# A new written order for the first nineteen steps of attention + MoE on one core, with two products moved to other banks

## The chip, the cores and the metric

The kernel runs on one core of a Trainium2 chip. The time is device microseconds (us) of one execution; the number given for a kernel is the median of its runs. A profile is one execution with the hardware profiler on; its span runs from the first instruction to the last. PE is the matmul engine (PEld its weight loads), DVE the vector engine, ACT the scalar engine with its tables, POOL the general one, SP the engine that only issues DMAs here.

## The reference

```python
def _attn_ref(q, k, v):                       # (8, 8, 576, 64) each
    q_s = softmax of q over the last axis
    k_s = softmax of k over the sequence
    kv = np.einsum('bhsd,bhse->bhde', k_s, v)
    return np.einsum('bhsd,bhde->bhse', q_s, kv)
def _moe_ref(x, w_in, w_out):                 # x: the result above as (4608, 512); w_in (512, 2048), w_out (2048, 512)
    h = x @ w_in
    g = h - np.tanh(h)
    return g @ w_out
```

Both softmaxes subtract the maximum first and divide by the sum + 1e-9. The weights come in 64 bit floats (512 KB for a 128-row piece) and are decoded on the chip.

## The kernel before

The 4608 rows of x are worked in nine chunks of 512. For each chunk j and each of 16 slices f of d_ff there is a **step** (j, f): a product `ph` = x times a slice of w_in (12 matmuls of 128x512, since x and the weight are split into a high and a low part: xh·wh, xl·wh, xh·wl), then the function of it, then `po`, the product of its result with a slice of w_out into four sums of 128 rows (12 matmuls, 3 for each sum), two steps later. The first steps are (0, 0) to (0, 7), then (1, 0) to (1, 15); step number n in the order's names is (0, n) for n < 8, else (1, n - 8). The sums of chunk 0 over its first eight slices are put aside in DRAM (`ev` copies a sum to SBUF, `sv` stores it) and taken up again later.

PSUM has eight banks here: four for the sums (`ps_o`, tag "o"), two for the products `ph` (`ps_h`, tag "h"), two for the rest (`ps_m`, tag "m"). Each pool hands its banks out in turn, so a tile waits until all readers of the tile that had its bank are done. Until the sums begin, the four banks of `ps_o` hold the first transposes and the first `px`.

Around the products stand small operations, one engine each:

- a step: `u`, `t`, `vv`, `m` (the mask `mk`), `gh` on ACT; `g`, `tt`, `gg`, `cp` on DVE; `gl` on POOL, or on DVE with a star in the order. `u`, `t`, `m`, `g`, `tt` read the product's bank.
- a weight piece, w_in (`i`) or w_out (`o`): `ld` is its load (SP), `cl` and `st` on DVE, `pr`, `lo` and `ca` on ACT, `sub` (the low part) on POOL, or on DVE with a star.
- k and v of a batch: loads `k`, `v` (the 512 KB pieces of v are filled with ones by POOL first), column maximum `km` on DVE, `pm` (transpose, PE), `mx`, `mh`, `ml` (DVE), `pb` (PE), `ks` (subtract, DVE), `ke` (exp, ACT), `pk` (PE), `sl`, `rs`, `rc`, `kn` (DVE), which gives `kvs`.
- a piece of q: load `q`, `mq` (maximum, DVE), `qu` (subtract, POOL), `qe` (exp, ACT), `sq` (sum, DVE), `sa`, `sr`; then per 128 rows `qn` (POOL), `pt` (transpose, PE), `qs` (copy, ACT), and per pair `px` (PE), whose parts `xh` (ACT) and `xl` (DVE) are x.

`warmN` is N idle matmuls on the identity. The string ORDER lists all of this for the first 17 steps, batches 0 and 1 and all 32 weight pieces, in one list; each engine executes its entries in that order, and its instructions wait only by semaphores. From step 17 on loops write the steps, PE and SP in order and the others as a scheduler orders them; batch 2's k and v are worked among the last steps of ORDER.

Of the kernel before, what the change touches and what calls it, by code (L numbers as in the profile page):

```python
# [29 lines left out]


ORDER = """
k0.0 warm13 k0.1 q1 km0.a k0.2 km0.b q0 km0.c mq1 v0.1 km0.d qu1 pm0 v0.2 mq0 warm16 v0.0 mx0
qu0 qe1 ld.i0 sq1 qe0 ld.o0 mh0 sa1 ml0 sr1 pb0 sq0 qn2 ld.i2 warm1 lo.i0 qn3 ks0.0 pt2 warm1
qs2 sa0 pt3 ks0.1 ke0.0 ld.i1 warm2 qs3 ks0.2 pk0.0 ke0.1 sr0 ld.i3 cl.i0 qn0* pr.i0 pk0.1 cl.i2
ke0.2 st.i0 pr.i2 ld.o2 pt0 cl.i1 ca.i0 qn1 pk0.2 lo.i2 warm1 sl0 sub.i0 pr.i1 ld.i4 rs0 pt1 rc0
qs0 warm2 kn0 qs1 cl.i3 px2 lo.i1 cl.o0 ld.o1 st.i2 pr.o0 px0 st.i1 xh2.1 cl.o2 xh2.0 xl2.1
ld.i5 ca.i1 warm11 xl2.0 xh0.1 xh0.0 sub.i1* ca.i2 xl0.1 ld.o3 lo.o0 sub.i2 xl0.0 pr.i3 ph0
lo.i3 k1.0 cl.o1 lo.o1 st.o0 lo.i4 st.i3 ca.o0 cl.i4 ld.o4 cl.o3 ca.i3 sub.o0* pr.i4 ph1 sub.i3*
u0 st.i4 k1.2 t0 ld.i6 vv0 g0 m0 tt0 ca.i4 gg0 ph2 v1.0 u1 sub.i4 t1 g1 vv1 tt1 lo.o2 ld.i7 gg1  # L40
pr.o2 cp0 u2 st.o2 pr.o1 k1.1 cl.i6 gh0 st.o1 m1 gl0* t2 ph3 q3 cp1 ca.o2 ca.o1 cl.i5 sub.o2*
gh1 sub.o1 g2 pr.i5 ld.o5 tt2 m2 po0 t3 gl1* vv2 v1.2 km1.a pr.i6 v1.1 gg2 pr.o3 km1.b u3 ph4
cp2 lo.o3 ld.o6 g3 lo.i5 st.o3 gh2 lo.i6 st.i5 q2 ca.o3 gl2* po1 ca.i5 st.i6 vv3 sub.i5* ld.o7
ca.i6 gg3 m3 sub.o3 tt3 lo.i7 mq3 ld.i8 po2 lo.o5 sub.i6 u4 mq2 t4 vv4 ld.i9 qu3 g4 lo.o4 ph5
tt4 lo.o7 lo.o6 ld.o8 cp3 qe3 km1.c gh3 cl.o4 ld.o12 km1.d m4 t5 sq3 gl3 ph6 pr.o4 ld.o11 u5 tt5
lo.i9 cl.i7 lo.i8 gg4 ld.o13 pr.i7 st.o4 po3 vv5 cp4 ca.o4 st.i7 ld.i12 gh4 qu2* u6 m5 pm1 gl4*
qe2 ld.i11 mx1 ca.i7 sub.o4* t6 sq2 sub.i7 po4 ld.o9 lo.o11 lo.i12 g5 lo.o8 mh1 cl.o5 lo.o13
ld.o10 ml1 gg5 pr.o5 sa2 pb1 sa3 cp5 vv6 sr2 ld.i10 lo.i11 sr3 ph7 qn5 ks1.0 gh5 m6 gl5 ks1.1
ke1.0 ld.i13 ks1.2 lo.o9 qn6 pk1.0 ke1.1 tt6 qn7 g6 pt6 ke1.2 pk1.1 qs6 st.o5 ld.o15 t7 qn4*
ca.o5 pt5 cl.o6 pk1.2 u7 sub.o5* qs5 ld.i15 sl1 gg6 po5 pr.o6 rs1 lo.i13 cp6 vv7 rc1 st.o6 gh6  # L50
kn1 ca.o6 cl.o7 pt4 m7 g7 sub.o6 pt7 qs4 tt7 qs7 gl6* pr.o7 px6 lo.o15 gg7 lo.i15 st.o7 po6
ld.i14 xh6.0 cp7 xh6.1 xl6.0 gh7 xl6.1 ca.o7 gl7* lo.o10 px4 sub.o7* lo.i10 lo.o12 cl.i8 cl.i9
po7.0 xh4.1 ld.o14 cl.o8 xh4.0 cl.o9 po7.1 xl4.1 pr.i8 xl4.0 pr.i9 po7.2 st.i8 pr.o8 ph8 st.i9
ev.1 ca.i8 cl.o11 sv.1 cl.i11 ca.i9 sub.i8 pr.i11 lo.o14 po7.3 sub.i9* t8 ph9 cl.i13 u8 tt8 m8
g8 vv8 cl.i10 ev.3 gg8 pr.i10 sv.3 cl.o14 ev.2 cp8 ph10 t9 sv.2 st.i10 gh8 tt9 m9 gl8* u9 pr.o14
st.o8 po8.0 t10 g9 vv9 po8.1 tt10 u10 gg9 ph11 ca.o8 g10 vv10 cp9 pr.o9 gg10 gh9 sub.o8* m10
po8.2 gl9* t11 ph12 u11 cp10 ev.0 g11 m11 sv.0 tt11 vv11 cl.o12 ca.i10 gg11 pr.o11 po8.3
sub.i10* u12 ph13 cp11 gh10 st.o11 vv12 gl10* m12 st.i11 t12 pr.o12 g12 po9 t13 tt12 u13 gg12
ca.i11 tt13 vv13 sub.i11 lo.i14 ph14 gh11 cp12 ca.o11 gl11 m13 pr.i13 sub.o11 g13 po10 u14 t14
gg13 tt14 vv14 cp13 ph15 st.o12 gh12 cl.i14 m14 gl12* ca.o12 cl.o15 pr.i14 g14 pr.o15 st.i14  # L60
po11 u15 gg14 t15 sub.o12* ca.i14 cp14 vv15 tt15 m15 ph16 sub.i14* gh13 cl.i12 gl13* pr.i12
st.o14 g15 ca.o14 po12 st.i12 t16 u16 gg15 ca.i12 sub.o14 tt16 vv16 cp15 gh14 sub.i12 m16 gl14*
st.o15 po13 g16 ca.o15 gg16 cl.o10 cp16 po14 gh15 cl.o13 sub.o15 pr.o10 pr.o13 gl15* st.o10 gh16
st.o13 ca.o10 gl16 ca.o13 sub.o13* sub.o10* st.o9 cl.i15 ca.o9 pr.i15 sub.o9 st.i15 st.i13
ca.i15 ca.i13 sub.i15 sub.i13
"""


# [1 line left out]
def attn_moe_kernel(  # L70
# [113 lines left out]

# [351 lines left out]
    po = {}

    def h_mm(j: int, f: int):
        xh, xl = xs[j]
        ph = ps_h.tile([P, CH], F32, name=f"ph{j}_{f}", tag="h")  # L540
        w = wt["i", f].rearrange("p t (c f) -> p t c f", c=NC)
        ops = [(i, x, c) for i, x in ((0, xh), (0, xl), (1, xh)) for c in range(NC)]
        for n, (i, x, c) in enumerate(ops):
            nc.tensor.matmul(  # L544
                ph, w[:, i, c], x[:, c, :], start=(n == 0), stop=(n == len(ops) - 1)
            )
# [281 lines left out]
```

## Time and profile before

| | |
|---|---|
| median of 3 runs | 918.2 us (917.87 to 918.79) |
| the profiled execution | 920.28 us, span 918.5 us |
| PE busy | 890.2 us (97%) |
| DVE, ACT, POOL busy | 615.4, 556.1, 288.2 us |
| first product `ph0` begins | 30.52 us into the span |
| `po16` ends, `ph19` begins | 159.45 us |
| weight pieces, q, k, v | 512 KB loads, 256 KB for each store of 128 rows |

In the rows of the profile, the name ahead of "<-" is what is written, behind it what is read, buffer numbers left out; xN is the number of instructions. In a table by stretches each engine has its busy us and, in brackets, its instructions; then follow the clock that PE was granted (1.00 is full), the DMA engines' share and GB/s. In a list of waits the columns are the total, the number and the longest, in us. A timeline row starts with the start and the length in us, and the bracket at its end holds the idle time before it and what ended it.

### The profile page before, as it was taken

The page shows a single profiled execution, that of the slowest core. Times are in us where ns is not written, and L with a number is a line of the kernel's source. Part 1 is how long each engine was busy: PE and PEld are TensorE (multiplying, and loading weights), DVE is VectorE, ACT ScalarE, POOL GpSimd, SP SyncE. Part 2 cuts the span into 40 slices and gives each one's busy share as a digit, 9 for nine tenths or more (in the row PEclk, how much of TensorE's full clock was granted, in tenths as well). Part 3 has the DMA queues.
Part 4 walks back from the last instruction along what each step waited for, and adds up shares of the span by engine and source line. Part 5 has one row for each costly group of instructions (what it writes and reads, how often), then busy time and mean ns, then how long its engine had stood idle before and what let it go on. Part 6 is the DMA issues. An engine that isn't in the chain of part 4 may idle for free.

```text
span 918.5 us, 13209 instructions
## 1 busy us (share of the span) xinstructions
PE 890.2 (97%) x5034; PEld 721.9 (79%) x5034; DVE 615.4 (67%) x906; ACT 556.1 (61%) x967; POOL 288.2 (31%) x246
## 2 busy tenths in 40 slices
...
GB/s 254 317 305 118 95 82 1 9 61 92 1 126 47 103 1 58 115 12 24 46 61 67 24 46 24 115 0 16 79 24 1 1 70 12 0 1 46 1 1 46
DMA packets 79776, 57.47 MB, mean 63 GB/s; under 512 B 14689, under 2 KB 72033, under 8 KB 79713
## 3 DMA queue, kind: packets, MB, share of 16 engines
...
q8 instruction: 39, 0.64, 0.3%
q14 instruction: 25, 0.20, 0.1%
...
## 4 chain that ended last, share of the span: by engine, by line
PE 77%; DVE 7%; ACT 5%; DMA 4%; issue 4%; POOL 2%; SPq 0%; DVEq 0%; ACTq 0%; POOLq 0%
PE po L635 37%; PE ph L544 35%; PE pk L299 2%; DMA k<-in_k_dram 2%; PE px L465 1%; PE pt L437 1%; DVE g L573 1%; DVE g L565 1%; DVE g L578 1%; DMA spare_q<-in_q_dram 1%; ACT gh L581 1%; DVE t L570 1%; DMA raw_o<-in_moe_w_out_dram 1%; POOL d L267 1%; DMA q<-in_q_dram 1%
## 5 line engine op out<-in xcount | busy, mean ns | idle before, releaser
L635 PE MATMUL po<-w_o,gh 128*128 128x512 f32 x1152 | 361.5, 395 | 1.5 <-DVE w_o L167 1.5
L544 PE MATMUL ph<-xh,w_i 128*128 128x512 f32 x1152 | 317.7, 398 | 10.3 <-ACT mk L559 6.0
L584 POOL TENSOR_TENSOR gl<-g,gh 128x512 fp32r<-128x512 f32 x130 | 172.6, 1328 | 389.7 <-ACT gh L581 373.5
L544 PEld LDWEIGHTS ph<-xh,w_i 128*128 128x128 f32 x1152 | 214.6, 190 | 59.3 <-ACT mk L559 7.3
L635 PEld LDWEIGHTS po<-w_o,gh 128*128 128x128 f32 x1152 | 214.7, 188 | 51.0 <-DVE w_o L167 1.8
L565 DVE SCALAR_TENSOR_TENSOR g<-u,ph 128x512 f32<-128x512 f32 x144 | 98.3, 682 | 219.2 <-ACT t L559 202.2
L635 PE MATMUL po<-w_o,gl 128*128 128x512 f32 x576 | 226.4, 393 | 1.5 <-DVE gl L584 1.5
L581 ACT CAST gh<-g 128x512 fp32r<-128x512 f32 x144 | 89.2, 620 | 177.7 <-DVE g L578 172.6
L544 PE MATMUL ph<-xl,w_i 128*128 128x512 f32 x576 | 157.9, 397 | 0.0
L559 ACT ACTIVATE u<-ph 128x512 f32<-128x512 f32 x144 | 85.8, 596 | 81.4 <-PE ph L544 81.1
L573 DVE SCALAR_TENSOR_TENSOR g<-vv,g 128x512 f32<-128x512 f32 x144 | 120.4, 836 | 20.0 <-ACT vv L559 10.4
L544 PEld LDWEIGHTS ph<-xl,w_i 128*128 128x128 f32 x576 | 109.8, 191 | 25.0 <-DVE xl L486 0.6
L635 PEld LDWEIGHTS po<-w_o,gl 128*128 128x128 f32 x576 | 108.1, 188 | 27.0 <-DVE gl L584 2.4
L578 DVE COPY_PREDICATED g<-mk,t 128x512 f32<-128x512 int32 x144 | 118.8, 825 | 3.3
L559 ACT ACTIVATE vv<-u,b_pa 128x512 f32<-128x512 f32 x144 | 104.5, 726 | 6.9 <-DVE g L573 6.8
L559 ACT ACTIVATE mk<-ph 128x512 int32<-128x512 f32 x144 | 86.2, 599 | 35.9 <-DVE g L565 32.3
L570 DVE TENSOR_TENSOR t<-ph,t 128x512 f32<-128x512 f32 x144 | 98.0, 681 | 4.0 <-ACT mk L559 3.1
L559 ACT ACTIVATE t<-ph 128x512 f32<-128x512 f32 x144 | 85.2, 592 | 1.1 <-PE ph L544 1.1
L389 POOL TENSOR_TENSOR q<-q,mq 128x1024 f32<-128x1024 f32 x14 | 27.7, 1979 | 47.5 <-DVE mq L384 44.6
L423 POOL TENSOR_TENSOR qn<-q,sq 128x512 f32<-128x512 f32 x28 | 31.9, 1142 | 28.1 <-DVE sq L403 14.6
L384 DVE TENSOR_REDUCE mq<-q 128x16 f32<-128x1024 f32 x15 | 18.2, 1216 | 23.9 <-DMA q<-in_q_dram 23.9
L167 POOL TENSOR_TENSOR w_i<-c_i,w_i 128x512 fp32r<-128x512 f32 x10 | 14.5, 1451 | 52.2 <-ACT w_i L163 42.6
...
## 6 DMA issues: line engine op xcount, KB each, us to landing
...
```

The source lines that it names most:

```text
L299: nc.tensor.matmul(st["pk"][hh * D : (hh + 1) * D, a, j : j + D + 1], kt[:, h, j] if u < NKP else kt[:, h], vt[:, h, j * (D + 1) : (j + 1) ...
L389: eng.tensor_tensor(qf, qf, mq, op=ALU.subtract)
L423: eng.tensor_tensor(qn.rearrange("p a g d -> p g a d"), qt[:, :, j].rearrange("p (g a) d -> p g a d", g=2), sq[:, :, j : j + 1] .broadcast ...
L544: nc.tensor.matmul(ph, w[:, i, c], x[:, c, :], start=(n == 0), stop=(n == len(ops) - 1))
L559: st["last"] = nc.scalar.activation(new(tag, **of), st[src], fn, **kw)
L565: nc.vector.scalar_tensor_tensor(new("g"), st["u"], C2, st["ph"], op0=ALU.mult, op1=ALU.mult)
L570: nc.vector.tensor_tensor(st["t"], st["ph"], st["t"], op=ALU.subtract)
L573: nc.vector.scalar_tensor_tensor(st["g"], st["vv"], PB, st["g"], op0=ALU.add, op1=ALU.mult)
L578: nc.vector.copy_predicated(st["g"], st["mk"], st["t"])
L581: nc.scalar.copy(new("gh", F32R), st["g"])
L584: eng.tensor_tensor(new("gl", F32R), st["g"], st["gh"].bitcast(F32), op=ALU.subtract)
L635: nc.tensor.matmul(po[t], g[:, cols], wt["o", f][:, w], start=(begin and n == 0), stop=(end and n == 2),)
```

## The change

ORDER is written anew and covers 19 steps (0 to 18) instead of 17. The same entries stand in it otherwise, with these differences in number: 25 idle matmuls instead of 47; the subtraction `qu2` and one of the `qn` are POOL's instead of DVE's; sixteen `sub` on DVE instead of fifteen; the two steps more bring their own entries. The products of steps 2 and 3 take banks of `ps_o`, and idle matmuls behind the first x take a bank of `ps_o` too.

```diff
 ORDER = """
-k0.0 warm13 k0.1 q1 km0.a k0.2 km0.b q0 km0.c mq1 v0.1 km0.d qu1 pm0 v0.2 mq0 warm16 v0.0 mx0
+q0 q1 mq0 k0.0 qu0 mq1 km0.a k0.1 qu1 k0.2 q3 qe0 sq0 sa0 qe1 km0.b sr0 km0.c ld.i0 mq3 km0.d
...
     def warm(n: int):
 
-        t = ps_h.tile([P, P], F32, name="warm", tag="h")
+        pool, tag = ((ps_m, "m") if po else (ps_o, "o")) if xs else (ps_h, "h")
+        t = pool.tile([P, P], F32, name="warm", tag=tag)
         for _ in range(n):
             nc.tensor.matmul(t, ident, ident, start=True, stop=True)
...
     def h_mm(j: int, f: int):
         xh, xl = xs[j]
-        ph = ps_h.tile([P, CH], F32, name=f"ph{j}_{f}", tag="h")
+
+        pool, tag = (ps_o, "o") if j == 0 and f in (2, 3) else (ps_h, "h")
+        ph = pool.tile([P, CH], F32, name=f"ph{j}_{f}", tag=tag)
...
-    PLANNED, SPREAD = 17, 3
+    PLANNED, SPREAD = 19, 3
```

Where the new table moves instructions: first SP's loads, from the start of the program. In these names `k0_0` is batch 0, piece 0; `spare_q` is the second piece of q of batch 0, `spare_v` the second piece of v; `raw_i0` is weight piece i0. Before:

```order
L189 DMA k0_0_103<-in_k_dram 128x8x128
L189 DMA k0_1_119<-in_k_dram 128x8x128
L369 DMA spare_q_121<-in_q_dram 128x8x128
L194 DMA kr0_125<-in_k_dram 64x8x64
L369 DMA q0_0_128<-in_q_dram 128x8x128
L208 DMA spare_v_133<-in_v_dram 128x8x128
L214 DMA vr0_143<-in_v_dram 64x8x64
L208 DMA v0_0_165<-in_v_dram 128x8x128
L123 DMA raw_i0_172<-in_moe_w_in_dram 128x4x128
```

And after, from the start too:

```order
L375 DMA q0_0_103<-in_q_dram 128x8x128
L375 DMA spare_q_105<-in_q_dram 128x8x128
L195 DMA k0_0_109<-in_k_dram 128x8x128
L195 DMA k0_1_116<-in_k_dram 128x8x128
L200 DMA kr0_119<-in_k_dram 64x8x64
L375 DMA q1_1_121<-in_q_dram 128x8x128
L124 DMA raw_i0_131<-in_moe_w_in_dram 128x4x128
L124 DMA raw_i1_157<-in_moe_w_in_dram 128x4x128
L124 DMA raw_i3_161<-in_moe_w_in_dram 128x4x128
L220 DMA vr0_181<-in_v_dram 64x8x64
L214 DMA v0_0_213<-in_v_dram 128x8x128
L214 DMA spare_v_232<-in_v_dram 128x8x128
```

Both pieces of q are ahead of k; a piece of batch 1's q and three weight pieces are ahead of v; `spare_v` went from the sixth place to the twelfth, and behind it follow i2, i4 and, fifteenth, `q1_0`.

On DVE the low part of x (`xl0`) is the last that the first product needs. Before, from the factor `kvs0` on:

```order
L320 TENSOR_TENSOR kvs0_92<-pk0_229,rs0_304 128x256
L145 TENSOR_SCALAR raw_i3_248<-raw_i3_248 128x512
L145 TENSOR_SCALAR raw_o0_177<-raw_o0_177 128x512
L156 SCALAR_TENSOR_TENSOR c_i2_342<-raw_i2_198 128x512
L156 SCALAR_TENSOR_TENSOR c_i1_363<-raw_i1_222 128x512
L145 TENSOR_SCALAR raw_o2_275<-raw_o2_275 128x512
L486 TENSOR_TENSOR xl0_366<-px2_1_321,xh0_365 128x2x256
```

After, from the same place:

```order
L326 TENSOR_TENSOR kvs0_92<-pk0_237,rs0_322 128x256
L146 TENSOR_SCALAR raw_i2_254<-raw_i2_254 128x512
L146 TENSOR_SCALAR raw_i4_263<-raw_i4_263 128x512
L390 TENSOR_REDUCE mq1_0_391<-q1_0_281 128x16
L490 TENSOR_TENSOR xl0_370<-px2_1_339,xh0_369 128x2x256
L490 TENSOR_TENSOR xl0_370<-px2_0_338,xh0_369 128x2x256
```

The row maximum of `q1_0` (the entry `mq2`) now stands ahead of `xl0`.

On PE, the first products. Before, from `ph2` on (`ph0_2` is the product of step 2; the third row of a product, which reads like its first, is left out):

```order
L544 MATMUL ph0_2_467<-xh0_365,w_i2_391 128x512 x4
L544 MATMUL ph0_2_467<-xl0_366,w_i2_391 128x512 x4
L544 MATMUL ph0_3_517<-xh0_365,w_i3_429 128x512 x4
L544 MATMUL ph0_3_517<-xl0_366,w_i3_429 128x512 x4
L635 MATMUL po0_0_0_550<-w_o0_423,gh0_0_507 128x512 x2
```

After, from `ph4` on, which follows `ph2`, `pm1`, `ph3` and `pb1` (`pk1` and `pt5` belong to batch 1's attention):

```order
L548 MATMUL ph0_4_600<-xh0_369,w_i4_462 128x512 x4
L548 MATMUL ph0_4_600<-xl0_370,w_i4_462 128x512 x4
L548 MATMUL ph0_5_617<-xh0_369,w_i5_514 128x512 x4
L548 MATMUL ph0_5_617<-xl0_370,w_i5_514 128x512 x4
L305 MATMUL pk1_650<-v1_0_458,k1_0_304 64x65 x16
L443 MATMUL pt5_667<-ident_79,qn5_639 128x128 x4
L305 MATMUL pk1_650<-spare_v1_483,k1_1_306 64x65 x16
L305 MATMUL pk1_650<-vr1_319,kr1_314 64x65 x8
L639 MATMUL po0_0_0_719<-w_o0_488,gh0_0_574 128x512 x2
```

Six products and batch 1's `pm1`, `pb1` and `pk1` now come ahead of the first `po`, where four products did before.

More of the change, by code (lines that the diff above doesn't have):

```diff
@@ L32 @@
 ORDER = """
-k0.0 warm13 k0.1 q1 km0.a k0.2 km0.b q0 km0.c mq1 v0.1 km0.d qu1 pm0 v0.2 mq0 warm16 v0.0 mx0
[L34 to L62, printed above, removed]
@@ L63 @@
-st.o15 po13 g16 ca.o15 gg16 cl.o10 cp16 po14 gh15 cl.o13 sub.o15 pr.o10 pr.o13 gl15* st.o10 gh16
-st.o13 ca.o10 gl16 ca.o13 sub.o13* sub.o10* st.o9 cl.i15 ca.o9 pr.i15 sub.o9 st.i15 st.i13
-ca.i15 ca.i13 sub.i15 sub.i13
+q0 q1 mq0 k0.0 qu0 mq1 km0.a k0.1 qu1 k0.2 q3 qe0 sq0 sa0 qe1 km0.b sr0 km0.c ld.i0 mq3 km0.d
+sq1 warm13 pm0 ld.i1 mx0 ld.i3 qn0 lo.i0 qu3 mh0 ml0 cl.i1 sa1 cl.i0 lo.i1 qe3 sr1 qn1* pr.i1
+lo.i3 v0.2 warm5 pb0 pt0 cl.i3 ks0.0 ks0.1 pt1 pr.i0 v0.0 pr.i3 qn2 ke0.0 qn3 ke0.1 warm2 pt2
@@ new lines @@
+ks0.2 v0.1 warm1 pk0.0 ld.i2 ke0.2 st.i1 st.i3 st.i0 ld.i4 pk0.1 q2 ca.i1 sub.i1 ld.o0 ca.i3 sq3
+pk0.2 sl0 ca.i0 k1.0 k1.1 pt3 qs2 k1.2 sa3 ld.i5 v1.2 rs0 rc0 qs3 sr3 kn0 qs1 sub.i0 qs0 cl.i2
+lo.i4 warm3 px2 cl.i4 qn6 ld.i7 ld.o4 ld.o1 ld.o2 qn7 xh2.1 xh2.0 px0 mq2 xh0.1 xh0.0 lo.i2
+pr.i4 xl2.1 pt7 xl2.0 xl0.1 qu2 pr.i2 pt6 xl0.0 qs7 lo.o0 warm1 ph0 st.i4 st.i2 km1.a sub.i3*
+ld.i6 ca.i2 ph1 cl.o0 km1.b sub.i2 v1.0 qe2 ca.i4 u0 sq2 pr.o0 g0 lo.i5 cl.i5 t0 km1.c pr.i5
+ld.o5 vv0 u1 v1.1 st.o0 ca.o0 st.i5 ld.o3 km1.d g1 ph2 gg0 tt0 ld.o7 ca.i5 qs6 t1 pm1 mx1 ld.i8
@@ new lines @@
+cl.o1 mh1 m0 sa2 ph3 ml1 u2 sr2 vv1 lo.o1 pb1 ld.o6 pr.o1 lo.i7 sub.i4 cp0 tt1 ld.o15 cl.o4 gh0
+gg1 cl.o2 m1 t3 ld.o12 sub.o0 vv2 cp1 gh1 st.o1 ld.o8 lo.o2 ld.i11 t2 ks1.0 ph4 ks1.2 sub.i5 gl0
+ph5 g2 u3 ks1.1 ke1.0 gl1 ke1.2 qn5 m2 tt2 gg2 cp2 ke1.1 pr.o2 g3 pk1.0 pt5 tt3 pk1.1 cl.o5 u5
+pk1.2 cl.i7 sl1 m3 cl.i6 ca.o1 st.o2 ld.i9 vv3 qs5 ld.i12 lo.o3 po0 qn4 pt4 pr.i6 cl.o3 ca.o2
+lo.i6 sub.o1* rs1 gh2 pr.o3 t4 cl.o7 qs4 gg3 pr.o4 rc1 u4 st.i6 ca.i6 pr.i7 vv4 lo.o5 kn1 gl2*
+cp3 m4 po1 px4 xh4.0 sub.o2* g4 sub.i6 tt4 ld.i13 st.o3 ld.o13 gg4 po2 st.i7 gh3 xh4.1 cp4 ca.o3
```

25 lines of the change are left out of this document (22 added, 3 removed).

## The prediction

> **What bounds the kernel now.** I read the page first, then the span cut into three stages, then who ended PE's and DVE's waits in the middle one, then timelines. The page's first row shows PE near full overall:
>
> ```profile
> PE 890.2 (97%) x5034; PEld 721.9 (79%) x5034; DVE 615.4 (67%) x906; ACT 556.1 (61%) x967; POOL 288.2 (31%) x246
> ```
>
> That average hides where time can be won. The cut is made at the first product (`ph0`, 30.52) and behind `po16` (156.73 to 159.45), the last step of the after order:
>
> ```profile
> 30.52 1.21 PE L544 MATMUL ph<-xh,w_i 128*128 128x512 f32 x4
> 156.73 0.62 PE L635 MATMUL po<-w_o,gh 128*128 128x512 f32 x2
> ...
> 159.45 1.07 PE L544 MATMUL ph<-xh,w_i 128*128 128x512 f32 x4
> ```
>
> ```profile
> core 0: us, PE busy (x) PEld busy (x) DVE busy (x) ACT busy (x) POOL busy (x), PEclk, DMA share, GB/s
> 0.00:30.52 30.52, 23.26 (x266) 22.02 (x267) 20.40 (x36) 15.16 (x24) 10.82 (x19) 0.89 0.98 284
> 30.52:159.45 128.93, 116.85 (x606) 91.22 (x605) 117.93 (x191) 107.84 (x194) 32.51 (x28) 0.96 0.47 141
> 159.45:918.50 759.05, 750.04 (x4165) 608.67 (x4163) 477.06 (x681) 433.06 (x751) 244.88 (x200) 1.00 0.15 40
> ```
>
> Behind 159.45 PE idles 9.0 of 759.05 us, in code that the change leaves alone. In the middle stage PE idles 12.1 us, DVE only 11.0 and ACT 21.1. Who ended PE's waits there, and the slower matmuls:
>
> ```profile
> PE ph L544 <- ACT mk L559: 6.0, 3, 2.2
> PE ph L544 <- DVE t L570: 2.0, 1, 2.0
> PE po L635 <- DVE gl L584: 1.5, 2, 1.3
> PE po L635 <- DVE w_o L167: 1.5, 1, 1.5
> 35.80:39.20 3.40, 1.41 (x7) 0.84 (x6) 2.70 (x4) 3.25 (x7) 0.87 (x1) 1.00 1.13 302
> 39.20:42.60 3.40, 3.40 (x10) 2.62 (x9) 3.40 (x6) 1.90 (x4) 0.41 (x1) 0.50 1.15 304
> 46.00:49.40 3.40, 3.40 (x10) 2.62 (x9) 3.40 (x7) 2.52 (x5) 1.56 (x3) 0.50 0.04 11
> 114.30:117.70 3.40, 3.40 (x10) 2.64 (x9) 2.74 (x6) 2.83 (x6) 0.00 (x0) 0.50 0.20 80
> 62.00:66.50 4.50, 2.85 (x13) 2.05 (x12) 4.50 (x8) 3.25 (x7) 2.73 (x2) 1.00 1.04 378
> ```
>
> Most of the waiting is `ph` for readers of a product two steps back (`mk`, `t`): two banks of `ps_h`. Three stretches of 3.4 us ran at clock 0.50; the stretch before the first had PE busy for 1.41 us of 3.40. A stretch with 2.85 of 4.50 was followed by none. At half clock half the work is done, so the three cost 3 x 1.7 = 5.1 us. PE's own need in the stage is therefore 116.85 - 5.1 = 111.8 us, against 128.93 spent.
>
> DVE's waits show that it is nearly a second bound:
>
> ```profile
> DVE g L573 <- ACT vv L559: 1.6, 1, 1.6
> DVE g L565 <- ACT mk L559: 1.4, 2, 0.7
> DVE km L223 <- DMA k<-in_k_dram: 1.1, 1, 1.1
> DVE km L226 <- DMA k<-in_k_dram: 1.0, 1, 1.0
> 50.00:80.00 30.00, 26.88 (x122) 21.19 (x121) 28.62 (x44) 28.64 (x50) 11.22 (x8) 1.00 0.80 279
> 60.00:80.00 20.00, 16.88 (x80) 13.13 (x78) 19.88 (x34) 18.65 (x32) 7.77 (x6) 1.00 0.68 246
> ```
>
> So a better order can win PE's losses only as far as DVE can be packed.
>
> **The first product, later.** Both kernels' first six loads are five of 512 KB and one of 128. Before, the sixth (`spare_v`) lands at 13.9; after, the sixth is `q1_1`, and `km0.d` and thus `pm0` stand behind its row maximum on DVE.
>
> ```profile
> L208 SPq DMA_DIRECT2D spare_v<-in_v_dram x1: 1736/1736/1736, 5.9 to 5.9; - x1
> DMA to landing us min/median/max: 8.0/8.0/8.0
> 9.22 1.22 DVE L384 TENSOR_REDUCE mq<-spare_q 128x16 f32<-128x1024 f32 x1 [0.84 <-DMA spare_q<-in_q_dram]
> 10.53 2.27 POOL L389 TENSOR_TENSOR spare_q<-spare_q,mq 128x1024 f32<-128x1024 f32 x1 [8.79 <-DVE mq L384]
> 15.78 2.05 POOL L423 TENSOR_TENSOR qn<-spare_q,sq 128x512 f32<-128x512 f32 x2 [0.74 <-DVE sq L403]
> L208 SPq DMA_DIRECT2D v<-in_v_dram x1: 368/368/368, 12.9 to 12.9; - x1
> DMA to landing us min/median/max: 4.2/4.2/4.2
> 22.19 1.15 PE L299 MATMUL pk<-spare_v,k 128*64 128x65 f32 x32 [0.28 <-ACT k L288]
> 25.19 0.43 DVE L320 TENSOR_TENSOR kvs<-pk,rs 128x256 f32<-128x256 f32 x1
> 28.53 1.29 DVE L486 TENSOR_TENSOR xl<-px,xh 128x512 fp32r<-128x512 f32 x2
> L123 SPq DMA_DIRECT2D raw_i<-in_moe_w_in_dram x1: 580/580/580, 17.7 to 17.7; - x1
> DMA to landing us min/median/max: 10.4/10.4/10.4
> ```
>
> After: maximum 13.9 + 1.2 = 15.1, `qu3` on POOL + 2.3 = 17.4, and behind it POOL's fills of `vr`, `v`; then, once `sr1` is there (18.8, behind `sq1`, `mx`, `mh`, `ml` and two clamps), `qn2`, `qn3` + 2.05 = 20.9; only then the fill that lets SP load `spare_v`, landing 4.2 later at 25.1. Its `pk` began at 22.19 before: 2.9 later. From there to `kvs` ready (25.62) took 3.4; without the transposes between I take 2.9, so 28.0.
>
> A second wait decides: on DVE `mq2` stands ahead of `xl`, and needs the fifteenth load. The fifteenth before, behind the same bytes, landed at 17.7 + 10.4 = 28.1; after, the queue first runs dry until 25.1, and three more 512 KB at some 317 GB/s (the page's third slice) take 5.0, so 30.1 (28.1 is the lower end). Then `mq2` 1.2, and two `xl` 1.2, which the last idle matmul waits for since it now takes the bank of the first `px`: 32.6, **first product at 32.8 instead of 30.52, +2.3**; `xl` is complete at 33.7, when `ph0` comes to it.
>
> **The banks.** `ph2` and `ph3` in `ps_o` wait for no reader. `ph4`, `ph5` stand behind `pm1`, `ph3`, `pb1`, so the readers of `ph0`, `ph1` have two products more. This takes the 2.0 and one or two of the 2.2 us waits, and with them two half-clock stretches: some 6 to 8 us of PE. `po0` of rows 2 and 3 now waits for `tt2`, `tt3`; by DVE's order these are behind `ks1`, ahead of `po0`'s other needs, so I cost that at nothing as long as `pk1` and `pt5` (2.9 us on PE) cover it.
>
> **DVE's work in the stage.** Three 1024-wide reductions (`mq3`, `mq2`, `sq3`; 1.14 from one start to the next, 9.22 to 10.36) are done before the first product: -3.4. `qu2` goes to POOL, -1.14, one `qn` -0.6; until `gl16` one `gl` less, -0.6, and `cp17` not yet, -0.64; one clamp more, +0.34. (A 512-wide operation counts 0.60 start to start: two `xl` in 1.29.) Sum -6.0: **117.9 - 6.0 = 111.9 us**. POOL takes what DVE loses; it is busy for 32.51 of 128.93. What that can cost is the neighbour's slowing:
>
> ```profile
> 38.33 1.28 POOL L167 TENSOR_TENSOR w_i<-c_i,w_i 128x512 fp32r<-128x512 f32 x1 [5.90 <-ACT w_i L163]
> 38.38 1.77 DVE L573 SCALAR_TENSOR_TENSOR g<-vv,g 128x512 f32<-128x512 f32 x1
> 41.28 0.68 DVE L573 SCALAR_TENSOR_TENSOR g<-vv,g 128x512 f32<-128x512 f32 x1
> ```
>
> 1.77 instead of 0.68 while POOL works, so up to 1.1 per POOL operation. Of such there are about as many after in this stage, and I leave the sum there; from 1.1 less for each of two to as much more, ±2.2.
>
> DVE's idle time: 11.0 before is the upper end. The densest stretch, 60 to 80, idles 0.12 of 20 (0.7 us over 111.9), 50 to 80 idles 1.38 of 30 (5.4). I take 3.0, between them, since the 2.1 for batch 2's k, which again is loaded behind the four `aside` stores, stays. `gl16`, now DVE's and nearly last in its written order, is then ready at 32.8 + 111.9 + 3.0 = 147.7, and `po16` ends about 2.6 later (it took 2.72, and its first two matmuls need `gh16` only); the product of step 19 that PE then has in its midst is counted apart. That is 150.3 for the 159.45 of before, **-9.1**.
>
> **Behind it.** `gl17` stands last, ten operations (6.1 us) behind `gl16`: 153.8; PE, with `ph19` (2.7), is at 153.0: +0.8. Nothing else moves.
>
> **Idle matmuls.** Before `pb0` 5 instead of 16, before `ph0` 1 instead of 11. They lay in waits for other engines; the removal itself wins nothing at `ph0`, where `xl` rules. The trace restored full clock only behind busy stretches, so the fewer are a risk (below). [...]
>
> **Sum.** -9.1 + 0.8 = -8.3. The profiled execution took 920.28, its span 918.5; the sum makes the span 910.2 and that execution 912.0. The median, 918.2, lies 2.1 below the profiled one, so the prediction is **909.9 us**.
>
> **Rivals.**
> - *PE alone bounds* (DVE never last): 32.8 + 111.8 = 144.6 for 159.45, -14.9: 903.3. For it: ACT idles 21.1 us, and POOL collisions may fall. Against: DVE's need alone is as long.
> - *DVE idles as before*, 11.0: eight us of the gain go, 917.9, no change that counts. For it: the ACT waits in DVE's list come from short dependence chains that an order may only move.
> - *Half clock at the first products.* The idle matmuls kept PE busy. With 22 fewer and waits of 2 us around `pk`, PE can be busy for under half of a stretch, and as in the rows above the next 3.4 us run at 0.50: +1.7 at the first products, so 911.6. [...]
> - *Slower: the load of `q1_0`.* Everything on DVE from `mq2` on is behind one load that SP issues fifteenth, and DVE is the bound, so each us late costs a us. It decides at 30.1 + 8.3 = 38.4: ten us behind the row of before. If SP stalls on the fill of `spare_v` and the q buffer together, say landing at 41, the time is 920.8. For it: SP's order is fixed, the fill hangs on POOL. Against: POOL's queue ahead of that fill adds up to 20.9; it would have to be near 29.
>
> **Chances.** Forecast (907 to 912.5) 0.50; PE bound or between (903 to 907) 0.18; half clock 0.07; partly lost (912.5 to 916.4) 0.09; idle as before 0.07; slower 0.09. A difference under 0.2% (1.8 us) can't be told from none here. Faster 0.84, same 0.07, slower 0.09. The range leaves out the last two and the far end of the PE-bound case: 903 to 916; the likeliest case alone 907 to 912.5.
>
> **What the profile after would show.** First product near 32.8, its wait ended by DVE `xl` behind `mq` <- DMA q; no `ph` wait before `ph4`; at most one 0.50 stretch; the end of `po16` near 153 with `ph19` ahead of it; DVE idle near 3 of the stage's 118. The prediction is wrong if DVE's idle stays near 11, if the first product comes after 36, or if PE is ahead of DVE everywhere.

## The result, and the profile after

The changed kernel is slower: 930.0 us (928.4 to 933.6) against 918.1 (917.9 to 918.8) for the kernel before, a ratio of 1.0134 (95% interval 1.0104 to 1.0164). The profiled execution took 929.8 us, its span is 928.0. The page's first row after; PE is less full than before:

```profile
PE 886.8 (96%) x4990; PEld 718.3 (77%) x4990; DVE 615.3 (66%) x906; ACT 556.1 (60%) x967; POOL 290.3 (31%) x246
```

With three steps of lag in the new order, `po16` and `ph19` are interleaved, so a cut that means the same work in both kernels is the start of `ph20`: 164.90 before, 176.57 after. From the first product to that point, by stretches, after:

```profile
core 0: us, PE busy (x) PEld busy (x) DVE busy (x) ACT busy (x) POOL busy (x), PEclk, DMA share, GB/s
33.63:176.57 142.94, 122.42 (x623) 95.21 (x622) 123.24 (x198) 111.06 (x202) 34.33 (x27) 0.95 0.42 129
176.57:928.00 751.43, 744.19 (x4141) 604.19 (x4139) 467.57 (x671) 428.00 (x740) 238.97 (x195) 1.00 0.15 41
```

and before:

```profile
30.52:164.90 134.38, 122.30 (x631) 95.69 (x629) 123.35 (x196) 111.97 (x201) 37.04 (x31) 0.96 0.46 136
164.90:918.50 753.60, 744.59 (x4141) 604.19 (x4140) 471.65 (x676) 428.93 (x743) 240.35 (x197) 1.00 0.15 41
```

DVE, ACT and PE are busy for nearly the same time as before (DVE 123.24 and 123.35, ACT 111.06 and 111.97, PE 122.42 and 122.30; POOL for 2.7 us less), but the stretch is 8.6 us longer. The loss is idle time: DVE 19.7 us instead of 11.0, PE 20.5 instead of 12.1. With the first product 3.1 us later, `ph20` is 11.7 late; behind it the new kernel is 2.2 shorter. That makes 9.5 us between the two spans; the medians are 12.0 apart, since the profiled execution of before was some 2 us above its median.

Who ended the waits between 33.6 and 177, after (total, number, longest, in us), on PE, on DVE and on ACT. The PE rows are the four longest. On DVE the wait of `cp` for its own mask (1.9) is left out; on ACT the waits of `vv`, `gh` and `ca` for DVE, which from 30 to 172 us are 4.6, 4.5 and 3.9 after and no shorter before (5.6, 5.8, 4.9), `u`'s for its product (3.0) and `gh`'s for PE (2.6):

```profile
PE ph L548 <- DVE g L569: 4.5, 1, 4.5
PE po L639 <- DVE gl L588: 4.2, 3, 1.7
PE ph L548 <- DVE t L574: 3.2, 2, 1.7
PE pm L241 <- DVE km L235: 2.6, 1, 2.6
```

```profile
DVE g L569 <- ACT mk L563: 3.3, 2, 3.0
DVE t L574 <- ACT mk L563: 3.1, 3, 2.3
DVE km L229 <- DMA k<-in_k_dram: 2.6, 1, 2.6
DVE g L569 <- ACT t L563: 1.9, 2, 1.2
DVE sq_rest L403 <- ACT q_rest L398: 1.6, 1, 1.6
```

```profile
ACT mk L563 <- DVE t L574: 2.9, 4, 1.3
ACT mk L563 <- DVE g L569: 2.8, 2, 2.0
ACT q_rest L398 <- POOL q_rest L395: 2.7, 1, 2.7
ACT t L563 <- DVE g L569: 2.3, 2, 1.8
```

Two kinds stand out. `g` (L569) reads `u` and the product, `tt` (L574, written `t`) the product and `t`; neither reads `mk`, yet both wait for it, 3.3 and 3.1 us in sum: in this profile the reads of one product by DVE and ACT came one behind the other, in the written order (up to step 18 the nearest two stand 0.03 us apart). The longest such wait is that of step 4, whose `g` waits for its `m`:

```profile
70.79 0.63 ACT L563 ACTIVATE mk<-ph 128x512 int32<-128x512 f32 x1
71.45 0.69 DVE L569 SCALAR_TENSOR_TENSOR g<-u,ph 128x512 f32<-128x512 f32 x1 [2.97 <-ACT mk L563]
```

Not all of this is new: ACT's `mk` waited for `tt` for 3.0 us before, too. The other kind is batch 2's first operations (`km`, `q_rest`, `sq_rest`), which wait in the midst of the steps. The two other long chains, batch 2's and the one at the end of the list, in rows of the timelines (the bracket is the idle time before a row):

```profile
117.53 0.69 DVE L229 TENSOR_TENSOR km<-k 128x512 f32<-128x512 f32 x1 [2.59 <-DMA k<-in_k_dram]
127.43 3.26 POOL L395 TENSOR_TENSOR q_rest<-q_rest,mq_rest 128x512 f32<-128x512 f32 x1 [3.63 <-DVE mq_rest L390]
130.72 0.63 ACT L398 ACTIVATE q_rest<-q_rest 128x512 f32<-128x512 f32 x1 [2.73 <-POOL q_rest L395]
135.87 1.65 PE L548 MATMUL ph<-xh,w_i 128*128 128x512 f32 x3 [4.47 <-DVE g L569]
171.41 1.29 DVE L588 TENSOR_TENSOR gl<-g,gh 128x512 fp32r<-128x512 f32 x2 [0.21 <-ACT gh L585]
172.76 0.79 PE L639 MATMUL po<-w_o,gl 128*128 128x512 f32 x1 [1.72 <-DVE gl L588]
```

The product of step 15 waits 4.5 us for `g` of step 13, which is behind ACT, which is behind POOL's subtraction for q's rest; and `po17` waits for `gl17`, the second of the two `gl` and the last entry on DVE.

The start of the products of some steps, in us, in the kernel before, after, and in five experiments below (read from PE's timelines):

| product of step | before | after | pin_after | readers_after | end_fix | v_early | repaired |
|---|---|---|---|---|---|---|---|
| 0 | 30.5 | 33.6 | 33.5 | 33.9 | 34.1 | 32.8 | 32.8 |
| 4 | 52.6 | 50.9 | 51.0 | 51.4 | 51.5 | 49.1 | 48.9 |
| 7 | 77.1 | 82.4 | 82.3 | 78.9 | 82.8 | 83.1 | 77.7 |
| 10 | 102.7 | 99.7 | 99.6 | 97.3 | 100.1 | 100.4 | 96.2 |
| 13 | 118.6 | 114.6 | 114.2 | 113.2 | 115.1 | 114.8 | 112.1 |
| 15 | 130.1 | 135.9 | 128.6 | 135.1 | 136.6 | 134.0 | 127.8 |
| 17 | 144.2 | 149.8 | 142.0 | 149.1 | 150.6 | 147.5 | 141.8 |
| 19 | 159.5 | 164.7 | 157.4 | 162.3 | 164.4 | 162.9 | 154.9 |
| 20 | 164.9 | 176.6 | 171.8 | 172.0 | 172.1 | 173.4 | 162.6 |

After begins late, is 4 us ahead at step 13, loses 9.7 us between steps 13 and 15, and 6.4 between 19 and 20.

### The profile page after: what moved, and what is told of

It is laid out like the page before. It is cut to its first block, busy times and chain, and to the rows that moved or that the text cites. A ratio compares the mean times of both kernels' runs of the same rounds, so it can differ in the third digit from the quotient of the medians.

```text
span 928.0 us, 13130 instructions
## 1 busy us (share of the span) xinstructions
PE 886.8 (96%) x4990; PEld 718.3 (77%) x4990; DVE 615.3 (66%) x906; ACT 556.1 (60%) x967; POOL 290.3 (31%) x246
## 4 chain that ended last, share of the span: by engine, by line
PE 78%; DVE 10%; ACT 7%; DMA 2%; issue 2%; SPq 1%; POOL 0%; ACTq 0%; DVEq 0%; POOLq 0%
PE po L639 37%; PE ph L548 35%; PE pk L305 2%; DVE g L582 2%; PE px L469 1%; PE pt L443 1%; DVE g L577 1%; DVE t L574 1%; ACT gh L585 1%; DVE g L569 1%; ACT t L563 1%; DMA k<-in_k_dram 1%; ACT u L563 1%; ACT mk L563 1%; ACT vv L563 1%
## 5 line engine op out<-in xcount | busy, mean ns | idle before, releaser
L548 PE MATMUL ph<-xh,w_i 128*128 128x512 f32 x1152 | 317.4, 398 | 11.7 <-DVE g L569 4.5
L569 DVE SCALAR_TENSOR_TENSOR g<-u,ph 128x512 f32<-128x512 f32 x144 | 98.3, 683 | 223.3 <-ACT t L563 211.4
L577 DVE SCALAR_TENSOR_TENSOR g<-vv,g 128x512 f32<-128x512 f32 x144 | 116.3, 808 | 18.3 <-ACT vv L563 8.0
L574 DVE TENSOR_TENSOR t<-ph,t 128x512 f32<-128x512 f32 x144 | 98.1, 682 | 6.2 <-ACT mk L563 4.9
L395 POOL TENSOR_TENSOR q<-q,mq 128x1024 f32<-128x1024 f32 x15 | 30.0, 2000 | 49.5 <-DVE mq L390 46.8
```

What stands on the lines that cost most here:

```text
L395: eng.tensor_tensor(qf, qf, mq, op=ALU.subtract)
L548: nc.tensor.matmul(ph, w[:, i, c], x[:, c, :], start=(n == 0), stop=(n == len(ops) - 1))
L569: nc.vector.scalar_tensor_tensor(new("g"), st["u"], C2, st["ph"], op0=ALU.mult, op1=ALU.mult)
L574: nc.vector.tensor_tensor(st["t"], st["ph"], st["t"], op=ALU.subtract)
L577: nc.vector.scalar_tensor_tensor(st["g"], st["vv"], PB, st["g"], op0=ALU.add, op1=ALU.mult)
```

## The experiments

Theory A: batch 2's early operations. B: the written order itself, DVE and ACT waiting for each other. C: the late start. D: a form of B, the order in which the two engines read one bank. E: the end of the list. The kernel before was run beside each group (918.0 to 918.9). Lines of the code differ by a few where an edit added one.

| kernel | median, us | ratio to before (95%) |
|---|---|---|
| pin_after | 927.0 | 1.0096 (1.0074 to 1.0117) |
| pin_before | 917.0 | 0.9987 (0.9976 to 0.9998) |
| tail_old | 922.8 | 1.0047 (1.0029 to 1.0064) |
| head_old | 936.8 | 1.0199 (1.0175 to 1.0222) |
| late_before | 922.9 | 1.0052 (1.0034 to 1.0069) |
| warm_gaps | 928.9 | 1.0118 (1.0076 to 1.0160) |
| mk2_after | 930.2 | 1.0122 (1.0087 to 1.0157) |
| bank_before | 916.1 | 0.9981 (0.9966 to 0.9996) |
| readers_after | 925.4 | 1.0080 (1.0060 to 1.0100) |
| readers_pin_after | 922.9 | 1.0053 (1.0035 to 1.0072) |
| bank_pin_before | 915.3 | 0.9973 (0.9962 to 0.9984) |
| all_before | 923.9 | 1.0060 (1.0041 to 1.0080) |
| v_early | 926.2 | 1.0098 (1.0067 to 1.0129) |
| end_fix | 925.1 | 1.0079 (1.0053 to 1.0105) |
| warm_old | 931.7 | 1.0150 (1.0118 to 1.0181) |
| repaired | 915.8 | 0.9976 (0.9960 to 0.9991) |
| three | 916.7 | 0.9993 (0.9979 to 1.0008) |
| repaired_mq2 | 917.4 | 0.9997 (0.9984 to 1.0011) |

**pin_after, pin_before.** Batch 2's operations are written by the loops behind ORDER; the scheduler puts them on DVE where it thinks them ready. The hold queues them on DVE behind `cp` of step 17:

```diff
-            nc.vector.copy_predicated(st["g"], st["mk"], st["t"])
+            held[j, f] = nc.vector.copy_predicated(st["g"], st["mk"], st["t"])
...
-                    call()
+                    with tc.issue_after(held[1, 9].ins):
+                        call()
```

> The new order, with only batch 2's small operations on DVE (km of batch 2, the maximum and sum of q's rest) held behind the mask-copy cp of step 17, so that they no longer stand between steps 11 and 14 in DVE's and ACT's queues. Theory A (batch 2's early operations make DVE and ACT wait: 2.6 us for its k, 1.6 for ACT behind POOL, then ph15 4.5 us late and 3.4 us of half-clock loss): 920 to 924. Theory B (the written order itself leaves DVE and ACT waiting for each other in the last eight steps): within 2 us of 930. Theory C (the late first product, the late pm1 and the half clock up to 50 us are the loss): within 2 us of 930 as well.

> The old order with the same hold for batch 2's operations. There DVE waited 1.1 and 1.0 us for k and 1.3 us behind POOL in this stretch, and one half-clock stretch followed at 114. Theory A: 914 to 916. Theories B and C: 917 to 919. If the operations come too late for pm of batch 2 (173 us before), slower than 918.

The product of step 16 came at 134.8 instead of 144.2, and there is no half-clock stretch at 135; of these 9.3 us 4.8 are left at step 20, where PE waits 4.4 us for `gl` (the end of the list, below) and 6.8 us at half clock from 165.5 lie on the way. The time went from 930.0 to 927.0, less than A expected; the intervals of the two ratios touch. On the old order the hold wins too (0.9987), by 1.7 us. So A is one cause, not the whole.

**tail_old, head_old.** ORDER is put together of both tables at `po5`, or at `ph0`; what is left follows in the other table's order, in `tail_old` with each `lo` directly ahead of its `pr`, and with `PLANNED` 17.

```diff
-gg7 pr.o12 po5 gh6 lo.o6 gl6* m7 t8 cp7 st.o6
+gg7 pr.o12 po5 ld.o9 lo.o6 st.o6 gh6 ca.o6 m7 sub.o6 gl6* po6 cp7 gh7
```

> The new order up to po5 (about 91 us), and from there the entries that are left in the old order, with 17 written steps. The new order was ahead there by 4 to 8 us at the products. Theory B: the lead is kept, 911 to 915. Theory A: as the old order, batch 2's operations come a little less badly, 913 to 918. Theory C: the loss lies in the head, 922 to 930.

> The old order up to ph0 (idle matmuls included), and from there the entries that are left in the new order, with 19 written steps and the two banks. First product again near 30.5 us, batch 1's k earlier. Theory C: most of the 12 us come back, 918 to 923. Theories A and B: the three us of the first product at most, 926 to 930.

`tail_old` took back 0.9% but is 0.47% slower than before. Its time, 922.8, lies in the range that I had given to C and not in those of A and B. Yet more than half of the loss went with the order behind `po5`, which is not where C puts it; as this edit also went back to 17 written steps, it does not place the loss exactly. The lead of 4 to 8 us in the products that I counted at `po5` was, as it seems, paid for on ACT: up to 80 us it had been busy for 56.1 us after, 59.6 before. `head_old` came out slower than any theory said and told nothing on C: in the mixture PE waited 10.1 us for one `qn` of POOL, a wait of a length that neither profile shows.

**late_before, warm_gaps, warm_old.** Only numbers of idle matmuls: 26 more ahead of `ph0` in the old order; 15 ahead of `pm1` and 30 ahead of `ph15` in the new; the old 16 and 11 in the new.

```diff
 late_before:  -pr.i3 ph0            +pr.i3 warm26 ph0
 warm_gaps:    -pm1 ... ph15         +warm15 pm1 ... warm30 ph15
 warm_old:     -warm5 pb0 ... warm1 ph0   +warm16 pb0 ... warm11 ph0
```

> The old order with 26 more idle matmuls (0.11 us each, 2.9 us) directly ahead of the first product, which then begins near 33.4 us instead of 30.5; nothing else is changed. Theory C (the late first product is carried to the end): 920.5 to 922. Theories A and B (DVE and ACT use the time for other entries, and the product is not what bounds the stage): within 1 us of before.

> The new order with idle matmuls in its two long waits of PE: 15 (1.7 us) ahead of pm1, 30 (3.3 us) ahead of ph15, so that the clock is kept there. If the half clock behind the waits is a cause of its own (1.7 us of work lost at 46, 3.4 at 135): 925 to 927. If the waits alone count, and the slower matmuls only use time in which PE would wait for DVE or ACT: 929 to 931. If the idle matmuls themselves come late: above 931.

> The new order with the old numbers of idle matmuls, 16 ahead of pb0 and 11 ahead of the first product (5 and 1 after). If the fewer idle matmuls cost clock ahead of the first products: 927 to 929. If they have no part: within 1.5 us of 930. If they come late, since the last of them waits for xl here: 930.5 to 931.5.

The sizes of two of these were wrong: an idle matmul is two rows of 0.11 us, so the 26 made the first product 6.5 us later (37.0), not 2.9. Of the 6.5, 3.1 were left at step 20, and the time rose by 4.0 us, or 4.8 by the ratio: in the old order a late start is carried on by half or more, but not us for us. In `warm_gaps` the 30 took 6.9 us and made `ph15` later than it was (142.5); `spare_v` also landed at 28.2 instead of 25.4 in its profile, with nothing changed ahead of it. `warm_gaps` is no slower than after, though its first product is 3.7 us and `ph15` 6.6 us later, and the half clock at 46 and 135 is gone; the two effects are not separated, so the question on the half clock is not settled by it. `warm_old` is not faster: the 16 delay the transposes behind them, and the first product came at 37.7. To put the idle matmuls back wins nothing in the new order; what the fewer of them cost by themselves is not shown.

**mk2_after.** `m` of a step gets a second buffer.

```diff
-            m=lambda: act("mk", "ph", AF.Square, scale=M_SCALE, dt=I32, bufs=1),
+            m=lambda: act("mk", "ph", AF.Square, scale=M_SCALE, dt=I32),
```

> The new order with two buffers for the mask mk instead of one, so that m of a step (ACT) no longer waits for cp of the step before (DVE). Theory B in the form that DVE and ACT wait for each other through this one buffer (ACT waits 7 us in the stage with mk as the instruction that waits): 922 to 926. Theory B in the form that the short chain of one step (ph, u, vv, gg, cp, gh, gl) sets the pace: within 1.5 us of 930. Theory A says nothing of it: within 1.5 us of 930.

Nothing: 930.2, with step 20 at 176.3. The waits named `mk` are not for this buffer.

**bank_before.** One part of the change alone on the old order.

```diff
-        ph = ps_h.tile([P, CH], F32, name=f"ph{j}_{f}", tag="h")
+        pool, tag = (ps_o, "o") if j == 0 and f == 2 else (ps_h, "h")
+        ph = pool.tile([P, CH], F32, name=f"ph{j}_{f}", tag=tag)
```

> The old order with one part of the change alone: the product of step 2 in a bank of the sums (ps_o), where it waits for no reader of ph0. In the profile before, ph2 waited 2.0 us and ph3 2.2, and the half clock took two stretches of 3.4 us behind them. If the banks bring what the prediction says: 914 to 916. If the gain is spent on the next wait (ph4 for its bank, po0 for its sums): within 1 us of before.

0.9981: the bank of step 2 is worth 2.8 us in the old order, 3.9 at step 20, and the three half-clock stretches behind the first product are gone. A part is spent on the next waits; PE's waits between 28 and 80 in this kernel:

```profile
PE ph L545 <- ACT mk L560: 2.2, 1, 2.2
PE po L636 <- ACT mk L560: 1.6, 1, 1.6
```

**readers_after, readers_pin_after, all_before.** In each step `u`, `t` read the bank first, then `g`, `tt`, then `m`: 13 entries of the new order move by a few places, 15 of the old one (with the bank and the hold, `all_before`). One of them:

```diff
-u0 sq2 pr.o0 g0 lo.i5 cl.i5 t0 km1.c
+u0 sq2 pr.o0 t0 g0 lo.i5 cl.i5 km1.c
```

> The new order with 13 single entries moved by a few places, so that in every step ACT's u and t read the product's bank first, then DVE's g and tt, then ACT's m. In the profile g waited for mk, which it does not read (3.3 us, one of 3.0), tt for mk (3.1), g for t (1.9), and on ACT mk and t for g and tt (6.0): reads of one bank by the two engines go in the written order, 14.3 us of such waits between 30 and 172 where the old order has 9.3. Theory D (this alternation is most of the waiting left without batch 2's part): 923 to 927. Theory B in its other form (the short chain of one step): 929 to 932, since m and so cp come later.

> The same 13 entries moved, and batch 2's operations held behind cp of step 17 as well. Theories A and D together: 919 to 923. If D is nothing: as with the hold alone, 926 to 928.

> The old order with the product of step 2 in a bank of the sums and batch 2's operations held. Alone they gave 2.8 and 1.7 us; if they add up, as their places (30 to 60 and 110 to 135 us) say: 913.5 to 915. If the second takes what the first had already won: 916.

> The kernel of bank_pin_before with the order of the five readers as well (15 entries moved). There is less of this waiting in the old order (9.3 us against 14.3). Theory D: 911 to 913. If D is nothing or m comes too late: 914 to 918.

`readers_after` is at 1.0080, its interval below that of after; with the hold 1.0053, as the two together should give. So D held in its number. Its mechanism is not shown: the waits of `g` and `tt` for `mk` are gone, but others on the same banks took their place, and from 30 to 172 us all waits of DVE and ACT for a read of the same bank that they have no other need of sum up to 18.1 us, where after has 14.3. What is shown is that the order of these entries costs 5 us, not which of the waits does. Waits in `readers_after` from 33.6 to 172:

```profile
DVE g L568 <- ACT t L562: 4.2, 4, 2.5
ACT mk L562 <- DVE t L573: 6.1, 6, 2.5
ACT mk L562 <- DVE g L568: 5.5, 4, 2.1
PE ph L547 <- ACT mk L562: 8.2, 7, 2.9
```

The products of steps 7 to 12 begin 1.7 to 3.5 us earlier, and DVE idles 17.2 us instead of 19.7. On the old order the same rule costs 0.87% (1.0060 against 0.9973 without it), which I had expected under no theory. Which reader comes last matters; that "`m` last" is right is not shown, and for the old order it is wrong. The bank and the hold together give 0.9973, about their sum (0.0019 and 0.0013), and are the fastest form of the old order.

**v_early, end_fix, repaired.** One entry moved, two entries moved, and all four causes together (the hold behind `cp` of step 18).

```diff
 v_early:
-q0 q1 mq0 k0.0 qu0 mq1 km0.a k0.1 qu1 k0.2 q3 qe0
+q0 q1 mq0 k0.0 qu0 mq1 km0.a k0.1 qu1 k0.2 q3 v0.1 qe0
...
-ks0.2 v0.1 warm1 pk0.0
+ks0.2 warm1 pk0.0
 end_fix:
-ca.o11 sub.i14 cp17 t18 vv18 st.i13 po16 g18 sub.o11 tt18 gg18 m18 cp18 sub.o10* ca.i13 gh17
-gh18 sub.i13* gl18* gl17*
+ca.o11 sub.i14 cp17 gh17 t18 vv18 st.i13 po16 gl17* g18 sub.o11 tt18 gg18 m18 cp18 sub.o10* ca.i13
+gh18 sub.i13* gl18*
```

> The new order with one entry moved: v0.1 (POOL's fill of spare_v and its load) directly behind the load of q1_1, so that spare_v is loaded seventh instead of twelfth. pk on it would then no longer wait (2.0 us) nor run at half clock, and the first product would come near 31 instead of 33.6. Theory C (the late first product is carried on, at the half that late_before showed): 928 to 929. If all of it is carried on: 927. If DVE, with its entries ahead of xl, hides it: 930.

> The new order with two entries moved: gh17 directly behind cp17 and gl17 behind po16, instead of last. Theory E (the end of the list: po17 waits for gl17, 1.7 us in the profile after, 3.3 where the other causes are taken away): 927 to 928.5. If PE's waiting only moves to the next product: 930.

> The new order with all four: v0.1 early, the readers' order, batch 2's operations held behind cp of step 18 (the last written step), gh17 and gl17 early. If these four are the whole cause: 916 to 919, no slower than the old order. If something else in the new order costs as much as what is still missing: 921 to 923.

`end_fix` won 5 us (1.0079), more than expected; PE's waits for `gl` from 160 on, after and in `end_fix`:

```profile
PE po L639 <- DVE gl L588: 3.0, 2, 1.7
PE po L638 <- DVE gl L587: 0.2, 1, 0.2
```

Up to step 19 it runs as after (164.4, 164.7), and step 20 comes 4.5 us earlier, with no half clock at 172: E is a cause, shown by itself in the trace, though the interval of its ratio just touches that of after.

`v_early` won 3.8 us (the intervals overlap), but not where it was meant to. Its first product came only 0.8 earlier, and steps 7 to 14 are no earlier than after. It differs at POOL's subtraction for q's rest:

```profile
126.63 1.44 POOL L394 TENSOR_TENSOR q_rest<-q_rest,mq_rest 128x512 f32<-128x512 f32 x1 [2.43 <-DVE mq_rest L389]
128.10 0.63 ACT L397 ACTIVATE q_rest<-q_rest 128x512 f32<-128x512 f32 x1 [0.91 <-POOL q_rest L394]
134.01 1.20 PE L547 MATMUL ph<-xh,w_i 128*128 128x512 f32 x4 [2.64 <-DVE g L568]
```

1.44 us instead of 3.26, so ACT waits 0.9 instead of 2.7 and step 15 comes 1.9 us earlier; no half clock follows there. That is theory A's place again, reached by chance, as far as one profile of each shows.

`repaired` runs at 0.9976: all four together win 14 us, make the new order faster than the old one, and leave no half-clock stretch behind the first product.

**three, repaired_mq2.** `three` is `repaired` without `v_early`. `repaired_mq2`:

```diff
-px0 mq2 xh0.1 xh0.0 lo.i2 pr.i4 xl2.1 pt7 xl2.0 xl0.1 qu2 pr.i2 pt6 xl0.0 qs7
+px0 xh0.1 xh0.0 lo.i2 pr.i4 xl2.1 pt7 xl2.0 xl0.1 pr.i2 pt6 xl0.0 mq2 qu2 qs7
```

> The repaired kernel without v_early: readers' order, batch 2's operations held behind cp of step 18, gh17 and gl17 early. If v_early won its 3.8 us only by where POOL's subtraction for q's rest fell among DVE's operations, which the hold moves away anyway: within 1 us of repaired (915.8). If the first part of the program matters by itself (first product, pk at half clock): 917.5 to 919.5.

> The repaired kernel with mq2 and qu2 (maximum and subtraction of q1_0) directly behind xl0 instead of ahead of it: DVE's xl and the first product begin 1.1 us earlier, nothing else is changed. If the first product is carried to the end: 914.5. If DVE's work, which stays the same, sets the end: within 0.5 us of repaired. If q of batch 1 then comes late (qe2, pt4, px4 hang on it): slower.

`three` is at 916.7 (0.9993), 0.9 us from `repaired` by the medians and 1.6 by the ratios, whose intervals overlap: with batch 2 held, the load of `spare_v` matters for less than these runs can tell from nothing. `repaired_mq2` made the first product 0.7 us earlier (32.1) and was no faster (0.9997, 1.6 us above `repaired` by the medians). It did not hold the rest fixed: `mq2` behind `xl0` pushed `km1` back by 1.9 us on DVE, so `pm1` waited 5.3 us instead of 2.6, at half clock (mean clock of the profile 0.988, 0.994 in `repaired`), and step 3 came 2.3 us later. Already in `repaired` PE waits 2.6 us for `km1` after three products; a first product that is earlier by less only lengthens this wait. So the first product's time, by which I had moved the whole stage us for us, is not by itself what the stage hangs on.

## Why the prediction was wrong, point by point

**The term that failed: DVE's idle time, 3.0 us.** Measured over the stretch to `ph20` it is 19.7, above even the upper end that I gave (11.0). I had read the densest 20 us of the old profile as what an order can reach over a whole stage. No kernel here reaches it; the lowest from the first product to `ph20` is 8.6 us, in `bank_pin_before`. `repaired`, the best form of the new order, over the same stretch:

```profile
32.80:162.64 129.84, 116.21 (x622) 90.75 (x622) 116.63 (x189) 108.75 (x200) 31.23 (x27) 1.00 0.43 138
```

DVE idles 13.2 us, PE 13.6, ACT 21.1. Neither DVE nor PE alone bounds: DVE and ACT execute their lists in order and wait for each other by the short chains of a step, so an entry that is late on one stops the other: in `repaired` DVE idles more than before (13.2 against 11.0) and the stretch is 4.5 us shorter all the same. My rival "DVE idles as before" named these chains, and priced them as if an order could only move them; this one lengthened them. Three places were shown:

- *Batch 2's operations.* I let "the 2.1 for batch 2's k" stay. After, DVE waited 2.6 for k and 1.6 for ACT, ACT 2.7 for POOL, and PE 4.5, with two half-clock windows behind it. The hold gives 9.3 us at step 16 and 3.0 at the end. I had left POOL's collisions as ±2.2 spread over the stage; one subtraction on POOL, in front of ACT, that was 1.8 us longer than in `v_early` (3.26 against 1.44) went with a wait of PE that was as much longer (4.47 against 2.64).
- *The readers of a bank.* I took a product's readers to wait for PE alone. They also wait for one another, and 13 moved entries took the ratio from 1.0134 to 1.0080, 5.0 us; by which of these waits stays open. In the trace `g` waited up to 3.0 us for `mk`, which it does not read; what makes one engine's read wait for the other's is not shown. Had I priced these waits, the order of five entries per step would have been a term of the sum.
- *The end of the list.* "+0.8" for `gl17`: I counted ten DVE operations at 0.61 us behind `gl16`, as if none of them waited. `gl16` began at 164.2, `gl17` at 172.0, 7.8 us later instead of 6.1; PE, ready for `po17` at 169.9, lost 2.1 us to `gh17` and `gl17`, and the 3.4 us from 172.4 ran at half clock behind them, which by an estimate (half of 3.4) is 1.7 more. By `end_fix` the right size was 5 us.

In ratios, the three alone take back 0.0038, 0.0054 and 0.0055; together (`three`, with the hold one step later) 0.0141, about their sum and as much as the loss of 0.0134. The single ones have intervals that touch that of after, except the readers; the sum does not.

**DVE's work, -6.0.** It left the front of the stage, but brought no gain. The first row of the stages after:

```profile
0.00:33.63 33.63, 20.21 (x230) 18.93 (x231) 24.51 (x38) 17.04 (x26) 17.02 (x25) 0.80 0.94 253
```

Ahead of the first product DVE is busy for 24.51 us instead of 20.40, 4.1 more, and behind `ph20` for 467.57 instead of 471.65, 4.1 less. So 4.1 us had left the stage at its front, and as `ph20` was late, as much of the following work was done ahead of it: 123.24 against 123.35. In `repaired`, whose `ph20` is not late, the stretch holds 116.63, 6.7 less than before: near the 6.0, though I had summed to `gl16` and not to `ph20`.

**The first product, +2.3.** It came 3.1 late. The chain up to `spare_v` was right: filled at 21.1, landed 4.1 us behind an issue at 21.3. (The 317 GB/s that I took for the loads behind it stand in the page's second slice; the third has 305, which makes 0.2 us.) Behind it two rows differ, on PE and on DVE, after:

```profile
25.51 1.94 PE L305 MATMUL pk<-spare_v,k 128*64 128x65 f32 x32 [2.01 <-ACT w_i L164]
29.51 2.00 DVE L146 TENSOR_SCALAR raw_i<-raw_i 128x512 f32<-128x512 f32 x2
31.43 1.21 DVE L390 TENSOR_REDUCE mq<-q 128x16 f32<-128x1024 f32 x1
32.56 2.47 DVE L490 TENSOR_TENSOR xl<-px,xh 128x512 fp32r<-128x512 f32 x4
```

`pk` ran at half clock (1.94 instead of 1.15), and `mq` did not wait for the load of `q1_0` (landed 30.7, forecast 30.1) but for two clamps that took 2.0 us. What was wrong is the use of this term: I let it carry on us for us, as DVE was to be the bound. `late_before` carried half or more, `three` against `repaired` less than can be measured; what the 3.1 us cost in the new order was not separated.

**The banks.** Right in mechanism: `ph2` and `ph3` waited for no reader, and `bank_before` wins with half of the edit (step 2 alone). Mis-sized: "6 to 8 us" were 2.8 there. In the new order the wait that took their place is in the words of the prediction itself, "`pm1`, `ph3`, `pb1`" ahead of `ph4`: `pm1` waited 2.6 us for `km1` on DVE, which I had not priced, and one of the half-clock stretches stayed.

**Behind the stage** nothing was lost in the profiled pair: 751.4 us from `ph20` instead of 753.6.

**The rivals.** None was the result. The slower one put its mechanism at the load of `q1_0`, 7.7 us from where it would have decided. The half clock came, at `pk` (25.6 to 29.0) instead of the first products.

**The clock.** I had two rows of the old profile, a stretch with PE busy for 1.41 of 3.40 us that half clock followed and one with 2.85 of 4.50 that none did. The runs show more of what lies between the two. The wait for `pm1` is 2.6 us in after and in `v_early`; the clock's windows lie differently. After:

```profile
39.28:42.69 3.41, 3.41 (x15) 2.45 (x14) 3.41 (x5) 1.33 (x3) 0.85 (x1) 1.00 1.05 385
42.69:46.10 3.41, 0.81 (x7) 0.80 (x7) 3.41 (x7) 3.41 (x8) 0.83 (x1) 1.00 1.08 360
46.10:49.52 3.42, 3.42 (x10) 2.68 (x9) 3.42 (x9) 2.38 (x6) 2.14 (x2) 0.50 1.12 333
```

and `v_early`:

```profile
40.02:43.43 3.41, 1.97 (x9) 1.29 (x7) 3.41 (x6) 1.68 (x4) 0.00 (x0) 1.00 1.09 364
43.43:46.85 3.42, 2.25 (x12) 1.99 (x13) 3.42 (x5) 2.58 (x6) 2.27 (x2) 1.00 1.12 336
46.85:50.26 3.41, 3.21 (x18) 2.52 (x18) 3.41 (x11) 3.20 (x6) 0.73 (x1) 1.00 1.06 377
```

In after the gap fell into one window (PE busy 0.81 of 3.41) and the next ran at 0.50; in `v_early` a border cut the same gap (1.97 and 2.25) and the next ran at 1.00. The borders stand on one grid in each of the two profiles of before and after: the half-clock stretches up to 180 us begin at 8.48, 39.20, 46.02 and 114.29 before and at 8.56, 25.62, 46.10, 134.85 and 172.40 after, whole multiples of 3.41 us apart. In these two, from the end of the first half-clock stretch to 250 us, the windows after which the clock fell to 0.50 had PE busy for at most 1.64 us, and those after which it stayed at 1.00 for at least 1.66:

```profile
155.33:158.74 3.41, 1.66 (x8) 1.36 (x8) 2.37 (x4) 3.03 (x7) 0.00 (x0) 1.00 0.00 0
158.74:162.16 3.42, 2.16 (x10) 1.49 (x9) 3.32 (x5) 2.62 (x6) 1.72 (x1) 1.00 0.00 0
168.98:172.40 3.42, 1.64 (x6) 0.70 (x5) 2.93 (x5) 2.40 (x5) 0.00 (x0) 1.00 0.00 0
172.40:175.81 3.41, 3.05 (x7) 2.47 (x8) 3.02 (x5) 0.60 (x1) 0.00 (x0) 0.50 0.02 5
```

Two profiles fix no bound, and what the clock goes by is not shown.
